# Softmax sums of a whole batch in one PSUM bank by 128x32 column tiles, spread over partitions through DRAM, and fp32 idle matmuls at the front

## The chip, the cores and the metric

The kernel runs on one core of one Trainium2 chip. The metric is the device time of a whole execution in microseconds (us); the number that counts is the median over runs. TensorE is called PE, VectorE DVE, ScalarE ACT, GpSimd POOL and SyncE SP.

## What is computed

A low-rank attention (Linformer) is followed by a feed-forward layer with a maximum over three up projections. All inputs and the output are fp32; the kernel computes in bf16 with fp32 sums.

```
k_proj = einsum('ks,bhsd->bhkd', E, k)       # 1024 keys become 64
v_proj = einsum('ks,bhsd->bhkd', F, v)
scores = (q @ k_proj^T) / 8
attn   = exp(scores - max) / (sum + 1e-9)    # 64 columns per row
x      = attn @ v_proj                       # (b, h, s, d) -> (b s, h d)
out    = max(x @ w1, x @ w2, x @ w3) @ w_out
```

There are 8 batches, 8 heads, 1024 positions, 64 per head; the model width is 512, the hidden width 768. The kernel leaves out the maximum of the scores.

## The kernel before

**Tiling.** Work goes batch by batch. The 8 heads are taken as 4 pairs `g`. For a pair, `scores` (L193) makes the transposed scores of 1024 positions with four 64x64 matmuls into two PSUM banks: partitions hold 64 projected keys for either half `c` of the positions, and the two banks hold the two heads `hp`. ACT writes `pT`, the exponentials in bf16 (`exps`, L208). `sums` (L227) multiplies `pT` with a block of ones, which gives the sums already spread over the 64 partitions of a head, in two banks; `values` (L242) multiplies the same `pT` with the projected values `vp`, in two more banks. Both go through `pair_mm` (L214), four 64x64 matmuls each. `invert` (L230) takes the reciprocal on ACT as Ln and then Exp of the negative, and `scale_x` (L247) multiplies values by it on DVE and writes `xT`, the input of the feed-forward part. `za` issues sums, values, inversion and scaling of a pair together; `sc` issues the scores and puts their Exp into a list, `later`, that is run after the next copy on ACT.

**The feed-forward part** of a batch has two chunks `ch` of 512 positions. `up` (L548) runs 6 steps `jt` of 12 matmuls (L506; three banks, four slices `ct` of `xT` each). The first step of a chunk leaves the last slice of all three banks to its end. ACT copies the first bank (`h1s`, L564), DVE takes two maxima (L568, L516). `down` runs 4 steps `tt` of 6 matmuls (L603); from batch 1 on ACT copies the result to `o_sb`, and SP stores it after every second step.

**Order.** Every engine's instructions run in the order in which the program writes them. `plan(b)` says behind which step of batch `b` the attention work of the next batch is issued: the key `(ch, step)` has steps 0 to 5 for the ups and 6 to 9 for the downs. `kproj`, `vproj` and `kt` make the projected keys and values, `qd` copies the queries on DVE and has SP issue a transposing DMA (L331), `ld` loads a batch through POOL's queue (L189). A planner that runs while the program is built keeps clocks for PE, ACT and DVE and gives each PSUM user the bank that it holds to be free first (`bank`, `two`); on the chip semaphores decide.

**The front.** Until E, F and the first heads have landed, `idle` (L376) issues matmuls on a zeroed tile, `warm`, whose results nobody reads. Batch 0 has an order of its own.

For batches 4 to 7 (`n`), this was the order:

```
        out = {
            (0, 1): [za(n, 0), sc(n, 1)],
            (0, 3): [za(n, 1), sc(n, 2)],
            (0, 9): [za(n, 2), sc(n, 3)],
            (1, 3): [za(n, 3)],
        }
```

Of the kernel before, what the change touches and what calls it, by code (L numbers as in the profile page):

```python
# [15 lines left out]
def kernel(  # L16
# [33 lines left out]
    const = ctx.enter_context(tc.tile_pool(name="const", bufs=1))  # L50
    loads = ctx.enter_context(tc.tile_pool(name="loads", bufs=1))
    att = ctx.enter_context(tc.tile_pool(name="att", bufs=2))
    psum = ctx.enter_context(tc.tile_pool(name="psum", bufs=1, space=bass.MemoryType.PSUM))

    ET = mybir.EngineType
# [61 lines left out]

    ident = const.tile([P, P], BF16, name="ident")
    ones = const.tile([P, HALF], BF16, name="ones")
    warm = const.tile([P, 512], BF16, name="warm")  # L120
    w_sb = [const.tile([P, NCT, DF], BF16, name=f"w{i}_sb") for i in range(3)]
    wout_sb = const.tile([P, NJT, DO], BF16, name="wout_sb")

# [43 lines left out]
    load_kv(2, slice(2, 4))  # L167

    nc.scalar.preload_act_table_set("natural_log_exp_and_others")
    nc.vector.memset(warm, 0.0)  # L170
    make_identity(nc, ident)
    nc.vector.memset(ones, 1.0)

    load_w(0, slice(0, 2))
    load_kv(2, V2)
# [31 lines left out]

    def exps(b, g, lo, nsi, sc):  # L208
        t, ns, ready = sc
        pTs[b, g, lo] = att.tile([P, 2, CHUNK], BF16, name="pT", bufs=4)[:, :, 0:nsi * HALF]  # L210
        nc.scalar.activation(out=pTs[b, g, lo], in_=t, func=AF.Exp, scale=scale)  # L211
        runs("s", ready, 0.17 + nsi * 0.107, ns)

# [13 lines left out]
    def sums(b, g, lo, nsi):  # L227
        return pair_mm(b, g, lo, nsi, lambda rows, hp: ones[rows])

    def invert(b, g, lo, nsi, z):  # L230
        t, ns, ready = z
        zl = att.tile([P, 2, CHUNK], FP32, name="zl", bufs=1)[:, :, 0:nsi * HALF]
        nc.scalar.activation(out=zl, in_=t, func=AF.Ln)  # L233
        runs("s", ready, 0.17 + nsi * 0.107, ns)
        if nsi == SI:
            zi = att.tile([P, 2, CHUNK], FP32, name="zi", bufs=2)
        else:
            zi = att.tile([P, 2, CHUNK // 2], FP32, name="zi0", bufs=4)
        nc.scalar.activation(out=zi, in_=zl, func=AF.Exp, scale=-1.0)  # L239
        zis[b, g, lo] = zi, runs("s", ready, 0.17 + nsi * 0.107)  # L240
# [19 lines left out]
            f()  # L260
        later.clear()

    def sc(b, g, lo=0, nsi=SI):
        def f():
            t = scores(b, g, lo, nsi)
            later.append(lambda: exps(b, g, lo, nsi, t))
        return f

    def za(b, g, lo=0, nsi=SI, then=False):
# [103 lines left out]
        return f  # L373


    def idle(n):  # L376

        t, ns = bank()
        for _ in range(n):
            nc.tensor.matmul(out=t, lhsT=warm[:, 0:P], rhs=warm, start=True, stop=True)  # L380
        free[ns[0]] = pe(n * MM)

    def turn_ef():
        for i in range(2):
# [239 lines left out]
    def plan(b):  # L624
        n = b + 1
        if b == 0:
            c1 = (SPC, SPC)
            return {
                (0, 6): [za(0, 1, *c1), sc(0, 3, *c1)],
                (0, 7): [qd(1, 2), za(0, 2, *c1)],  # L630
                (0, 8): [za(0, 3, *c1)],
                (1, 0): [kproj(1)],
                (1, 1): [kt(1)],
                (1, 2): [vproj(1), ld(2)],
                (1, (3, "mid")): [sc(1, 0), sc(1, 1)],
                (1, 4): [za(1, 0), sc(1, 2)],
                (1, 5): [za(1, 1), sc(1, 3)],
                (1, 7): [za(1, 2)],
                (1, 8): [za(1, 3)],
            }  # L640
# [36 lines left out]
        if n + 2 < B:  # L677
            out[1, 1] += [ld(n + 2)]
        return out
# [61 lines left out]
```

The softmax here doesn't subtract the row's maximum and nothing guards it: scores larger than these inputs give would overflow.

## Time and profile before

| | us |
|---|---|
| median of 10 runs | 405.14 (404.59 to 405.54) |
| the profiled execution | 405.24 |
| its span, first to last instruction | 403.5 |
| PE busy | 394.9 (98%) |
| DVE busy | 202.9 (50%) |
| ACT busy | 189.4 (47%) |
| up matmuls (L506), busy | 258.0 in 1152 |
| down matmuls (L603), busy | 85.6 in 378 |
| sums matmuls (L220, on ones), busy | 13.7 in 144 |

Busy time of an engine is the time in which at least one of its instructions ran. Matmuls overlap, so the duration of one (379 ns for 512 columns) is more than its share of PE's time. In the rows below, a row of a timeline gives start, duration, engine, line, operation, output and inputs, and the count; in brackets stands the idle time before it and what ended it. A row of busy times by stretch gives the stretch, its length, then for PE, PE's weight loads, DVE, ACT and POOL the busy time with the number of instructions, and last PE's clock, the share of the 16 DMA engines and GB/s.

### The profile page before, as it was taken

What the parts mean: (1) busy time and instruction counts of PE and PEld (TensorE: products, weight loads), DVE (VectorE), ACT (ScalarE), POOL (GpSimd) and SP (SyncE); (2) the same over time, 40 slices, a digit from 0 to 9 for tenths busy, and PEclk for the clock granted to TensorE, in tenths of its full rate; (3) what the DMA queues carried; (4) which work ended last, traced back from release to release, by engine and by line L of the source; (5) the groups of instructions that cost most, each with busy time, mean ns of one, the idle gap of its engine ahead of it and who ended that gap; (6) DMA issues with size and microseconds to landing.
All of it is one profiled execution on the core that took longest, in us unless ns stands there. A gap on an engine that the chain in (4) does not pass through costs nothing.

```text
span 403.5 us, 5884 instructions
## 1 busy us (share of the span) xinstructions
PE 394.9 (98%) x2357; PEld 178.5 (44%) x2357; DVE 202.9 (50%) x313; ACT 189.4 (47%) x274; POOL 31.4 (8%) x44
## 2 busy tenths in 40 slices
PE   6999999999999999999999999999999999999996
PEld 2544444444444435444544445444544444444443
DVE  2338755762765527537353655626364363525251
ACT  2531537525672366555643555437535555432322
POOL 7440001001000100200110002000000000000000
PEclk8999999999999999999999999999999999999999
DMA  9999999959907994991799019950510202020202
GB/s 145 206 206 208 233 205 157 241 128 176 237 3 212 191 224 106 154 246 18 210 173 216 29 36 240 205 146 0 145 66 2 104 2 104 2 104 0 106 0 105
DMA packets 62667, 53.33 MB, mean 132 GB/s; under 512 B 30128, under 2 KB 58288, under 8 KB 62640
## 3 DMA queue, kind: packets, MB, share of 16 engines
q0 software_dynamic: 28512, 28.31, 44.3%
q1 hardware_dynamic: 33984, 24.51, 19.8%
q8 instruction: 18, 0.29, 0.3%
q10 hardware_dynamic: 144, 0.13, 0.1%
q14 instruction: 9, 0.07, 0.1%
HBM read 57.15 MB, written 16.78 MB: 183 GB/s over the span
## 4 chain that ended last, share of the span: by engine, by line
PE 92%; ACT 3%; DMA 2%; DVE 2%; issue 1%; SPq 0%; ACTq 0%; DVEq 0%
PE banks L506 61%; PE banks L603 19%; PE banks L220 4%; PE banks L284 3%; PE banks L200 2%; DMA ef_f<-in_F_dram 1%; ACT zl L233 1%; DVE xT L250 1%; ACT zi L239 1%; PE banks L380 1%; PE banks L409 1%; PE banks L295 1%; DMA out_dram<-o_sb 0%; PE banks L435 0%; ACT pT L211 0%
## 5 line engine op out<-in xcount | busy, mean ns | idle before, releaser
L506 PE MATMUL banks<-xT,w_sb 128*128 128x512 bf16 x1152 | 258.0, 379 | 0.4 <-DVE xT L250 0.2
L506 PEld LDWEIGHTS <-w_sb 128*128 128x128 bf16 x1152 | 109.5, 98 | 137.1 <-issue 11.2
L568 DVE TENSOR_TENSOR m<-banks,h1s 128x512 f32<-128x512 f32 x90 | 62.1, 690 | 84.4 <-ACT h1s L564 52.2
L564 ACT COPY h1s<-banks 128x512 f32<-128x512 f32 x90 | 52.5, 583 | 90.3 <-PE banks L506 88.2
L603 PE MATMUL banks<-wout_sb,hT 128*128 128x512 bf16 x378 | 85.6, 379 | 0.0
L250 DVE TENSOR_TENSOR xT<-banks,zi 128x1024 bf16<-128x1024 f32 (+1 forms) x36 | 39.8, 1106 | 73.6 <-ACT zi L239 52.4
L516 DVE TENSOR_TENSOR hT<-banks,m 128x512 bf16<-128x512 f32 x90 | 62.3, 692 | 10.4 <-PE banks L506 1.2
L99 ACT COPY o_sb<-banks 128x512 f32<-128x512 f32 (+1 forms) x56 | 32.6, 581 | 52.2 <-PE banks L603 52.1
L603 PEld LDWEIGHTS <-hT 128*128 128x128 bf16 x378 | 36.0, 98 | 45.2 <-issue 3.1
L233 ACT ACTIVATE zl<-banks 128x1024 f32<-128x1024 f32 (+1 forms) x36 | 33.5, 930 | 31.4 <-PE banks L220 30.5
L211 ACT ACTIVATE pT<-banks 128x1024 bf16<-128x1024 f32 (+1 forms) x36 | 33.2, 930 | 15.9 <-PE banks L200 15.9
L239 ACT ACTIVATE zi<-zl 128x1024 f32<-128x1024 f32 (+1 forms) x36 | 34.6, 962 | 1.1
L189 POOL DMA_DIRECT2D q_t<-in_q_dram x7 | 6.2, 880 | 201.3 <-DMA qT<-q_p 107.2
L220 PE MATMUL banks<-pT,ones 64*64 64x512 bf16 (+1 forms) x144 | 13.7, 374 | 0.7 <-DVE xT L250 0.3
L220 PE MATMUL banks<-pT,vp 64*64 64x512 bf16 (+1 forms) x144 | 13.3, 355 | 0.4 <-DVE vp L99 0.4
L200 PE MATMUL banks<-qT,kpT 64*64 64x512 bf16 (+1 forms) x144 | 13.3, 358 | 0.3 <-DVE m L568 0.3
L284 PEld LDWEIGHTS <-efT 128*64 128x64 bf16 x224 | 11.6, 110 | 3.2 <-issue 2.7
L220 PEld LDWEIGHTS <-ones 64*64 64x64 bf16 x144 | 4.4, 103 | 14.3 <-issue 14.2
L99 DVE CAST vp<-banks 64x256 bf16<-64x256 f32 (+1 forms) x18 | 7.1, 397 | 6.8 <-ACT vp L99 3.5
L99 DVE COPY q_p<-q_t 128x1024 bf16<-128x1024 bf16 x28 | 10.0, 419 | 0.0
L380 PE MATMUL banks<-warm 128*128 128x512 bf16 x21 | 8.5, 527 | 1.2 <-DVE warm L170 1.2
L99 ACT CAST vp<-banks 64x256 bf16<-64x256 f32 x14 | 5.1, 365 | 8.7 <-PE banks L284 8.5
(48 smaller groups left out, 103.3 us busy)
## 6 DMA issues: line engine op xcount, KB each, us to landing
out_dram<-o_sb SPq DMA_DIRECT2D x30, 512.0 KB, 3.5
q_t<-in_q_dram POOLq DMA_DIRECT2D x7, 1024.0 KB, 9.4
k_t<-in_k_dram POOLq DMA_DIRECT2D x7, 1024.0 KB, 13.7
v_t<-in_v_dram POOLq DMA_DIRECT2D x7, 1024.0 KB, 19.0
w_sb<-in_moe_w_dram POOLq DMA_DIRECT2D x5, 384.0 KB, 12.0
k_t<-in_k_dram POOLq DMA_DIRECT2D x2, 512.0 KB, 9.0
v_t<-in_v_dram POOLq DMA_DIRECT2D x4, 256.0 KB, 12.4
wout_sb<-in_moe_w_out_dram POOLq DMA_DIRECT2D x1, 768.0 KB, 15.9
```

The lines of the kernel that those rows point to most:

```text
L99: done = {"v": nc.vector.tensor_copy, "s": nc.scalar.copy, "g": nc.gpsimd.tensor_copy}[eng](out=o, in_=i)
L211: nc.scalar.activation(out=pTs[b, g, lo], in_=t, func=AF.Exp, scale=scale)
L220: nc.tensor.matmul(out=t[hp * HALF:(hp + 1) * HALF, c, 0:nsi * HALF], lhsT=w(rows, hp), rhs=p[rows, hp, :], start=True, stop=True,)
L233: nc.scalar.activation(out=zl, in_=t, func=AF.Ln)
L239: nc.scalar.activation(out=zi, in_=zl, func=AF.Exp, scale=-1.0)
L250: nc.vector.tensor_tensor(out=xTs[b][:, g, lo:lo + nsi, :].rearrange("a (c s) p -> a c (s p)", c=2), in0=t, in1=zi, op=ALU.mult,)
L284: nc.tensor.matmul(out=t[hh * HALF:(hh + 1) * HALF, 0:width], lhsT=efT[:, si, (kv - 1) * KP:kv * KP], rhs=qkv[b][kv][:, heads[hh], si, :], ...
L506: nc.tensor.matmul(out=h, lhsT=w_sb[i][:, ct, jt * P:(jt + 1) * P], rhs=xTs[b][:, ct, ch * SPC:(ch + 1) * SPC, :], start=(ct == first), st ...
L516: nc.vector.tensor_tensor(out=o, in0=h, in1=other, op=ALU.max)
L564: nc.scalar.copy(out=h1s, in_=h[0][0])
L568: nc.vector.tensor_tensor(out=m12, in0=h[1][0], in1=h1s, op=ALU.max)
L603: nc.tensor.matmul(out=o_ps, lhsT=hTs[b, ch][:, jt, tt * P:(tt + 1) * P], rhs=wout_sb[:, jt, :], start=(jt == 0), stop=(jt == NJT - 1),)
```

## The change

Two edits.

At the front, `idle(10)` and `idle(4)` on the bf16 tile become `idle(3, warm_f)` and `idle(1, warm_f)` on an fp32 tile of the same shape, which DVE zeroes first. The planner counts such a matmul as four.

From batch 2 on, the sums of all four pairs are made together by `zc`. A matrix `pick` of zeros and ones has, for either head of a pair, 32 columns of which 8 sum the upper and 8 the lower half of the partitions. Four pairs use the four 32-column tiles of PE and write to the four partition quarters of one bank; the two heads accumulate one after the other. One Ln and one Exp of 128x512 follow on ACT. SP then stores one of every eight equal rows, 16 rows of 2 KB, to a scratch tensor in DRAM, waits for it, and loads it back in two DMAs, one per head half, each read by 64 partitions: 64 x 16 KB, 1 MB each. The result is `zi_all`, of one buffer. `vx` issues the values of a pair and their scaling. The order of work is written anew: the scores of a batch come two or three behind one step, some with their Exp at once (`now=True`), then `zc`, and the values some steps later, two pairs behind one step. `pT` gets six buffers instead of four. Batch 1 still uses `invert`, into a part of its `zi_all`; batch 0 is as before but for the front.

```diff
-        pTs[b, g, lo] = att.tile([P, 2, CHUNK], BF16, name="pT", bufs=4)[:, :, 0:nsi * HALF]
+        pTs[b, g, lo] = att.tile([P, 2, CHUNK], BF16, name="pT", bufs=6)[:, :, 0:nsi * HALF]
...
+    nc.vector.memset(warm_f, 0.0)
     nc.vector.memset(warm, 0.0)
     make_identity(nc, ident)
     nc.vector.memset(ones, 1.0)
+    nc.vector.memset(pick, 0.0)
+    for hp in range(2):
+        for c in range(2):
+            at = hp * 16 + c * 8
+            nc.vector.memset(pick[c * HALF:(c + 1) * HALF, hp, at:at + 8], 1.0)
...
+    def zc(b):
+        def f():
+            t, ns = bank()
+            for hp in range(2):
+                for g in range(NPAIR):
+                    nc.tensor.matmul(
+                        out=t[32 * g:32 * (g + 1), :], lhsT=pick[:, hp, :],
+                        rhs=pTs[b, g, 0][:, hp, :], start=(hp == 0), stop=(hp == 1),
+                    )
+            ready = pe(2 * MM + 0.1)
+            zlc = att.tile([P, CHUNK], FP32, name="zlc", bufs=1)
+            nc.scalar.activation(out=zlc, in_=t, func=AF.Ln)
+            runs("s", ready, 0.6, ns)
+            zic = att.tile([P, CHUNK], FP32, name="zic", bufs=1)
+            nc.scalar.activation(out=zic, in_=zlc, func=AF.Exp, scale=-1.0)
+            when = runs("s", ready, 0.63) + 9.0
+            zd = scratch.tile([NPAIR, 2, 2, CHUNK], FP32, name="zd")
+            nc.sync.dma_start(
+                out=zd.rearrange("g h c f -> (g h c) f"),
+                in_=zic.rearrange("(a r) f -> a r f", r=8)[:, 0, :],
+            )
+            for hp in range(2):
+                nc.sync.dma_start(
+                    out=zi_all(b)[hp * HALF:(hp + 1) * HALF],
+                    in_=zd[:, hp].partition_broadcast(HALF),
+                )
+            for g in range(NPAIR):
+                zis[b, g, 0] = zi_all(b)[:, g], when
+        return f
+
+    def vx(b, g):
+        def f():
+            scale_x(b, g, 0, SI, values(b, g, 0, SI))
+        return f
...
         if nsi == SI:
-            zi = att.tile([P, 2, CHUNK], FP32, name="zi", bufs=2)
+            zi = zi_all(b)[:, g]
...
-    idle(10)
+    idle(3, warm_f)
...
-    idle(4)
+    idle(1, warm_f)
...
-                (0, 7): [sc(2, 0)],
-                (0, 9): [za(2, 0), sc(2, 1)],
-                (1, 1): [za(2, 1), sc(2, 2)],
-                (1, 3): [za(2, 2), sc(2, 3)],
-                (1, 5): [za(2, 3)],
+                (0, 7): [sc(2, 0, now=True), sc(2, 1)],
+                (0, 9): [sc(2, 2, now=True), sc(2, 3)],
+                (1, 0): [zc(2)],
+                (1, 5): [vx(2, 0), vx(2, 1)],
                 (1, 6): [qd(3)],
+                (1, 7): [vx(2, 2), vx(2, 3)],
...
-                (0, 4): [sc(3, 0)],
-                (0, 6): [za(3, 0), sc(3, 1)],
-                (1, 0): [za(3, 1), sc(3, 2), qd(4)],
-                (1, 2): [za(3, 2), sc(3, 3), kproj(4), vproj(4), ld(5)],
+                (0, 4): [sc(3, 0, now=True), sc(3, 1)],
+                (0, 6): [sc(3, 2, now=True), sc(3, 3)],
+                (0, 8): [zc(3)],
+                (1, 0): [qd(4)],
+                (1, 2): [kproj(4), vproj(4), ld(5)],
+                (1, 3): [vx(3, 0), vx(3, 1)],
                 (1, 4): [kt(4)],
-                (1, 5): [za(3, 3), sc(4, 0)],
+                (1, 5): [vx(3, 2), vx(3, 3), sc(4, 0)],
...
-            (0, 1): [za(n, 0), sc(n, 1)],
-            (0, 3): [za(n, 1), sc(n, 2)],
-            (0, 9): [za(n, 2), sc(n, 3)],
-            (1, 3): [za(n, 3)],
+            (0, 1): [sc(n, 1, now=True), sc(n, 2, now=True), sc(n, 3)],
+            (0, 3): [zc(n)],
+            (1, 0): [vx(n, 0), vx(n, 1)],
+            (1, 3): [vx(n, 2), vx(n, 3)],
...
-            out[0, 9] += [kproj(n + 1), vproj(n + 1)]
+            out[1, 0] += [kproj(n + 1), vproj(n + 1)]
```

More of the change, by code (lines that the diff above doesn't have):

```diff
@@ L52 @@
     att = ctx.enter_context(tc.tile_pool(name="att", bufs=2))
+    scratch = ctx.enter_context(
+        tc.tile_pool(name="scratch", bufs=2, space=bass.MemoryType.DRAM)
+    )
     psum = ctx.enter_context(tc.tile_pool(name="psum", bufs=1, space=bass.MemoryType.PSUM))
@@ L119 @@
     ones = const.tile([P, HALF], BF16, name="ones")
+    pick = const.tile([P, 2, 32], BF16, name="pick")
     warm = const.tile([P, 512], BF16, name="warm")
+    warm_f = const.tile([P, 512], FP32, name="warm_f")
     w_sb = [const.tile([P, NCT, DF], BF16, name=f"w{i}_sb") for i in range(3)]
@@ L228, in sums, with zi_all @@
         return pair_mm(b, g, lo, nsi, lambda rows, hp: ones[rows])
+    zi_alls = {}
+    def zi_all(b):
+        if b not in zi_alls:
+            zi_alls[b] = att.tile([P, NPAIR, 2, CHUNK], FP32, name="zi_all", bufs=1)
+        return zi_alls[b]
+    def zc(b):
[23 more added lines that the diff above has]
+                    in_=zd[:, hp].partition_broadcast(HALF),
+                )
+            for g in range(NPAIR):
[5 more added lines that the diff above has]
+        return f
     def invert(b, g, lo, nsi, z):
@@ L261, in run_later, with sc @@
         later.clear()
-    def sc(b, g, lo=0, nsi=SI):
+    def sc(b, g, lo=0, nsi=SI, now=False):
         def f():
             t = scores(b, g, lo, nsi)
-            later.append(lambda: exps(b, g, lo, nsi, t))
+            if now:
+                exps(b, g, lo, nsi, t)
+            else:
+                later.append(lambda: exps(b, g, lo, nsi, t))
         return f
@@ L373, in vproj, with idle @@
         return f
-    def idle(n):
+    def idle(n, w=warm):
         t, ns = bank()
         for _ in range(n):
-            nc.tensor.matmul(out=t, lhsT=warm[:, 0:P], rhs=warm, start=True, stop=True)
-        free[ns[0]] = pe(n * MM)
+            nc.tensor.matmul(out=t, lhsT=w[:, 0:P], rhs=w, start=True, stop=True)
+        free[ns[0]] = pe(n * MM * (4 if w is warm_f else 1))
     def turn_ef():
```

## The prediction

> **What bounds the kernel now.** I read the page first (busy shares, the chain that ended last), then busy time by stretches, then the timeline around one attention stage.
>
> ```profile
> PE 394.9 (98%) x2357; PEld 178.5 (44%) x2357; DVE 202.9 (50%) x313; ACT 189.4 (47%) x274; POOL 31.4 (8%) x44
> ...
> PE 92%; ACT 3%; DMA 2%; DVE 2%; issue 1%; SPq 0%; ACTq 0%; DVEq 0%
> ...
> 80.00:120.00 40.00, 39.70 (x240) 17.82 (x239) 21.49 (x34) 21.00 (x29) 2.63 (x3) 1.00 0.74 143
> 120.00:160.00 40.00, 39.68 (x257) 18.70 (x255) 20.88 (x35) 19.56 (x30) 2.63 (x3) 1.00 0.86 185
> 160.00:200.00 40.00, 40.00 (x244) 18.07 (x242) 20.45 (x32) 22.04 (x31) 2.63 (x3) 1.00 0.76 156
> 200.00:240.00 40.00, 40.00 (x212) 17.55 (x211) 22.02 (x34) 19.65 (x28) 2.63 (x3) 1.00 0.57 108
> ```
>
> In the stretches the first number after the length is PE's busy time. The change acts from about 95 us on, and there PE idles 0.3 us in 80 to 120, 0.3 us in 120 to 160, then not at all. DVE and ACT are half idle. So only two things can move the time: PE work removed, and PE waits created. Time saved on ACT, which the change cuts most, is worth nothing where no PE wait ends on ACT. One stage shows what PE work costs:
>
> ```profile
> 178.01 0.41 PE L220 MATMUL banks<-pT,ones 64*64 64x512 bf16 x4
> ...
> 178.25 0.39 PE L220 MATMUL banks<-pT,vp 64*64 64x512 bf16 x4
> ...
> 178.47 0.39 PE L200 MATMUL banks<-qT,kpT 64*64 64x512 bf16 x4
> 178.53 1.02 ACT L233 ACTIVATE zl<-banks 128x1024 f32<-128x1024 f32 x1 [1.55 <-PE banks L220]
> ...
> 178.79 2.55 PE L506 MATMUL banks<-xT,w_sb 128*128 128x512 bf16 x11
> ```
>
> Four 64x64 matmuls start 0.22 us before the next four: they run side by side, so a group of four is worth 0.22 us. The next stage starts at 184.07, after 24 up matmuls (5.18 us on the chain), so the stage costs 6.06 - 5.18 = 0.88 us: three groups, 0.65, and 0.23 for going into the small tiles and out.
>
> **What the Trainium skill says.** "TensorE: Matmul & The Clock Gate", Part 3 (Packing small matmuls): outputs in different column tiles run concurrently; three 32-column tiles gave 2.38 times. The trace agrees for two column tiles: 32 projection matmuls (L284, 128x64, 256 columns) take 1.87 us, 0.117 a pair. Four are not shown. "SBUF — State Buffer", Door 1: a DMA to 64 partitions reached 196 GB/s at 1 MiB against 328 to 128, and "Can I just issue two DMAs to hit both halves?" says that two such DMAs gain only 6% together. No row here isolates this. "DMA: Bandwidth & Descriptors", Latency and other measured facts: streams whose rows lie at one large pitch in HBM fell to 103 GB/s, half the full rate. Reading one 4 KB row for 64 partitions may resemble that; no row here shows it.
>
> **The change, part by part.**
>
> *Sums on PE.* Removed per batch: four groups of sums, 4 x 0.22. Added: eight 128x32 matmuls in two rounds of four column tiles, 2 x 0.22 if all four run together; bounds 0.43 (as taken) and 8 x 0.216 = 1.73 (one after another). Batches 4 to 7 have four stages before (sums, values, scores) and four after (three scores; the sums; two values with the projections; two values and one scores), so 0.23 x 4 stays. Gain 0.43 a batch, 1.7 us for four.
>
> *Batch 2.* Twelve groups become ten in the same five stages: -0.43. The 0.3 us wait for pT near 98.3 goes. But the last Exp of the scores (1.03) is queued on ACT behind a down copy, another Exp and the h1s copy of an early step, which can start only after its tenth matmul. Laid out from 95.2: the second pair of scores ends at 99.05, the step at 101.65, h1s 101.4 to 102.0, Exp to 103.05, and the new sums need it: 1.3 us of PE wait. Net 1.3 - 0.43 - 0.3 = +0.6.
>
> *Batch 3.* Thirteen groups become eleven, five stages six (+0.23); the 0.3 us near 150.2, where scores waited for a bank, goes; the new sums follow the last scores by two downs and wait about 0.5 for the Exp. -0.43 + 0.23 - 0.3 + 0.5 = 0.
>
> *ACT and DVE.* Per batch four Ln (1.03) and four Exp (1.06) become one of each on 128x512 (0.60, 0.63 in the 128x512 rows): 7.1 us less ACT, hidden anyway. DVE does the same four products (1.23 each), now in pairs: 2.5 us in a step that has 2.59 - 1.38 = 1.2 us of DVE to spare. The banks cover that: after such a pair the next three banks are wanted at 0.9, 1.8 and 2.6 us, and are freed by then; DVE catches up in the next step. Three scores in a row take six banks, which ACT frees at 1.6, 2.6 and 4.2 us, while PE wants banks at 0.9 to 4.4 us: no wait.
>
> *The new wait.* The products now wait for two DMAs. With T the end of step (0,3): sums done T + 0.73, Ln and Exp to T + 2.1, then SP issues the store of 32 KB: nearest row 128 KB, 1.8 us; T + 4.0. SP waits for that landing, then issues two DMAs of 1 MB each to 64 partitions. Their price lies between two ends. As fast as stores: 512 KB lands in 2.6 us against 1.8 for 128 KB, so 2 MB in some 1.4 + 4.8 = 6.2 us. At the skill's rate for half the partitions, 2.1 MB at 208 GB/s (196 plus 6%) = 10.1, with 1.4 of latency 11.5. I take 11.5: landing T + 15.5. A third end is one hot row: at 103 GB/s some 22 us.
>
> Wanted: sums 0.66, two steps and four downs 10.4, step (1,0) 2.59 bring PE to T + 13.65; DVE ends that early step's last maximum 1.95 us later (200.54 to 202.49 in batch 3), so the product wants it at T + 15.6, and some 0.35 us later the projection copy behind it on DVE would hold PE's transposes. For batches 4 to 7, landing 15.5 against 15.6 to 15.95: no wait, but with a margin of under half a microsecond; what comes later than that is paid once a batch, for PE runs out of banks.
>
> *Queues.* Behind SP's waits stand the query transposes (4.0 us of issue) and stores; their data is wanted over 10 us later, o_sb has three buffers. Loads of batches 6 and 7 end before the sums do (DMA share 0.00 at 224 to 236). Not so in batch 2:
>
> ```profile
> 98.00:100.00 2.00, 1.70 (x17) 0.69 (x16) 0.00 (x0) 1.97 (x3) 0.00 (x0) 1.00 1.11 142
> 100.00:102.00 2.00, 2.00 (x11) 0.93 (x10) 0.83 (x1) 1.40 (x3) 0.00 (x0) 1.00 1.13 306
> ...
> 106.00:108.00 2.00, 2.00 (x11) 0.88 (x9) 0.71 (x1) 1.97 (x4) 0.00 (x0) 1.00 1.25 208
> 108.00:110.00 2.00, 2.00 (x11) 0.94 (x10) 1.81 (x4) 1.25 (x2) 0.00 (x0) 1.00 1.20 200
> 110.00:112.00 2.00, 2.00 (x19) 0.71 (x18) 1.38 (x2) 0.80 (x1) 0.00 (x0) 1.00 0.34 58
> ```
>
> The last two columns are DMA share and GB/s: the load of batch 3 keeps the engines full until 111, and stores issued in it took 7.1 to 7.6 us instead of 2.6. Sums end at 103.6, the small store goes out at 105.2, lands about 107.7; 11.5 more and some 1.8 for sharing: 121.0. PE wants it by about 118.5, since two products, four query copies (1.42) and two more products must be through before the next batch's third slice at 123.6. Wait 2.5 us (0 at the fast end, 13 or more at the hot end). Batch 3's transfer starts at 150.9, with the load over: landing 15.7 us after the start of its sums against 15.8. No wait.
>
> *The front.* Ten idle matmuls of 0.43 become three of four passes (four passes for true FP32: "FP8 and Floating Point Precision", TensorE Precision Notes; no row shows one): 12 x 0.43 = 5.1 from about 1.5, so ending by 6.6; the transposes wait for E and F until 7.08 anyway. The single one at 8.45 ends with its cover, the k load at 10.2. PE's clock column reads 0.50 at 9 to 11 us, after 1.9 us of idling; a busier front may avoid that: k_duo took 1.57 against 0.99 later, so 0 to -0.6. Bound the other way +0.6 if these passes keep the clock low for longer. I take -0.2.
>
> **Sum.** -1.7 + 0.6 + 0 + 2.5 - 0.2 = +1.2. The profiled execution took 405.24 (span 403.5), 0.1 above the median of 405.14: 405.14 + 1.2 = **406.3**.
>
> **Rivals.** (a) *The transfer comes in time everywhere*, near the fast end: batch 2's 2.5 goes, -1.3: 403.8, to 403.2 with a warm front. For it: stores move 4 KB pieces at over 400 GB/s. Against: they span 128 partitions. It decides when both DMAs land within 9 us of issue beside a load. (b) *The broadcast is slower than 11.5 us*, by hot rows or the port limit: each microsecond beyond 11.9 costs four batches one each, about as much for batches 2 and 3: 13 us gives 406.3 + 4 x 1.1 + 2.6 = 413; 16 us some 431. For it: a margin of 0.4; against: nothing else runs on the queues then. (c) *Column tiles do not overlap fourfold*: two at a time makes the sums worth nothing, +0.43 a batch, six batches: 409; one at a time 6 x 1.3 = +7.8: 414. Against it: L284. (d) *The front does nothing or harm*: within 0.6 of the forecast.
>
> **Chances.** Forecast as worked 0.40 (403.9 to 408.5 by its own bounds; 0.09 of it within 0.2% of 405.14, the rest slower); (a) 0.25, nearly all faster; (b) 0.27 slower; (c) 0.08, a part cancelled by (a) and so within 0.2%. Of these: faster 0.25, same 0.13, slower 0.62, where 0.2% (0.8 us) is about what a measurement of this kernel can tell from no change. Range 403.2 to 420: it leaves out a wholly warm and early case below and a broadcast of over 14 us above.
>
> **What would show it.** Right: the sums as eight matmuls starting within 0.25 us of each other by fours; the broadcast's time to landing 10 to 13 us; DVE's L250 products waiting on a DMA for 2 to 3 us in batch 2 and hardly later; PE still over 97% busy. Wrong: broadcast under 9 us (rival a), PE waits of over a microsecond at every (1,0) (b), L250 waiting on PE.

## The result and the profile after

The changed kernel is slower: median 417.73 us in 8 runs (416.31 to 418.60) against 405.19 in 29 runs of the kernel before, a ratio of 1.0305 (95% interval 1.0295 to 1.0314). The profiled execution took 417.68 us, its span 415.9.

First the page of the changed kernel: busy time by engine, TensorE's clock in 40 slices, the chain that ended last by engine, and the row of the two loads that spread the inverted sums (`zi_all`, from here on the spread), with the KB of each load and the median us from its issue to its landing.

```profile
PE 394.9 (95%) x2303; PEld 177.0 (43%) x2303; DVE 202.6 (49%) x319; ACT 149.3 (36%) x238; POOL 31.6 (8%) x44
...
PEclk9999999999996999999999999999999999999999
...
PE 62%; DMA 28%; DVE 3%; ACT 2%; issue 2%; POOL 1%; SPq 1%; DVEq 0%; ACTq 0%; POOLq 0%
...
zi_all<-zd SPq DMA_DIRECT2D x12, 1024.0 KB, 11.2
```

ACT has lost 40 us of work, as planned. PE is busy exactly as long as before although it has 54 matmuls less: some of its work ran at a lower clock. And DMA now holds 28% of the chain that ended last, where it held 2%. Not all of that is loss. Two loads of the front (`w_sb` 3.1%, `v_t` 7.2%) make up 10 of the 28 points, and they stand on the chain of e2 as well, which is faster than the kernel before. The spread has 12.8, the query transposes `qT` 3.4, the small store ahead of the spread 1.6. What these cost is read from PE's waits.

The same four stretches as before show where PE stands still; after the stretch and its length the first number is PE's busy time, and the third from the end its clock.

```profile
80.00:120.00 40.00, 38.73 (x222) 17.20 (x221) 17.35 (x29) 14.57 (x24) 2.63 (x3) 1.00 0.97 187
120.00:160.00 40.00, 34.27 (x190) 14.83 (x190) 16.08 (x25) 13.53 (x22) 2.63 (x3) 0.91 0.79 154
160.00:200.00 40.00, 38.95 (x230) 17.31 (x229) 23.00 (x36) 14.21 (x23) 2.63 (x3) 1.00 1.03 198
200.00:240.00 40.00, 36.76 (x217) 16.60 (x215) 18.53 (x29) 12.89 (x22) 2.63 (x3) 1.00 1.07 210
...
120.00:124.00 4.00, 0.00 (x0) 0.00 (x0) 0.00 (x0) 0.25 (x1) 0.00 (x0) 1.00 0.34 78
124.00:128.00 4.00, 2.27 (x12) 0.64 (x12) 3.55 (x6) 0.00 (x0) 0.00 (x0) 0.53 0.00 0
128.00:132.00 4.00, 4.00 (x13) 1.59 (x12) 2.41 (x3) 0.93 (x2) 0.00 (x0) 0.62 0.73 137
```

The loss is not spread over the batches. One hole lies at 120 to 124, a second, in the stretch from 200, at 211.6 to 214.4, and after the first the clock is about half. The timeline of the changed kernel names the instructions behind them; the bracket is the idle time before a row and what ended it.

```profile
102.73 0.59 PE L256 MATMUL banks<-pT,pick 128*32 128x512 bf16 x5 [0.90 <-ACT pT L222]
...
124.45 2.36 DVE L306 TENSOR_TENSOR xT<-banks,zi_all 128x1024 bf16<-128x1024 f32 x2 [7.34 <-DMA zi_all<-zd]
125.72 1.07 PE L231 MATMUL banks<-pT,vp 64*64 64x512 bf16 x8 [6.09 <-DVE xT L306]
...
176.81 0.41 PE L211 MATMUL banks<-qT,kpT 64*64 64x512 bf16 x4 [0.98 <-DMA qT<-q_p]
...
193.67 0.61 PE L256 MATMUL banks<-pT,pick 128*32 128x512 bf16 x8
...
214.40 1.02 PE L565 MATMUL banks<-xT,w_sb 128*128 128x512 bf16 x4 [2.80 <-DVE xT L306]
```

The eight sums matmuls of a batch take 0.61 us (193.67): four column tiles do run together. The product of batch 2 (124.45) waits 7.34 us for its inverses, and PE, out of banks behind it, 6.09 us. The product of batch 4 makes PE wait 2.80. How batch 2 comes to that is read down the chain of waits of the changed kernel (start, duration, what), which follows back from the last instruction to what released it:

```profile
104.65 5.03 DMA zd<-zic
...
110.40 13.93 DMA zi_all<-zd
...
124.45 1.24 DVE xT L306
...
126.79 4.83 PE banks L662 x12
...
162.46 14.31 DMA qT<-q_p
...
201.00 12.00 DMA zi_all<-zd
```

The store of 32 KB needs 5.03 us, the second of the two loads 13.93 from its issue. Then twelve down matmuls take 4.83 us that cost 2.59 elsewhere, at half the clock. The same chain later goes through the query transposes of batch 4, 14.31 us to landing, and the spread of batch 4, 12.00.

The chain also gives a balance between points where a fixed amount of PE work lies: from the first scores of batch 2 (95.23 us before, 95.00 after) to its first up matmul, and from there to the first up matmul of the next batch. The kernels below the second row are the experiments, each read from one profiled execution.

| kernel | batch 2: scores to first up | to batch 3's first up | to batch 4's first up |
|---|---|---|---|
| before | 27.42 | 50.25 | 47.00 |
| after | 36.62 | 50.88 | 50.07 |
| no transfer (e2) | 27.93 | 49.42 | 46.49 |
| spread in bf16 (e7) | 27.98 | 49.44 | 46.49 |
| load of batch 3 left out (e10) | 29.12 | 52.87 | 49.97 |
| part of that load earlier (e5) | 33.81 | 50.92 | 51.62 |
| wait filled (e8) | 33.48 | 52.03 | 53.04 |
| query copies earlier (e6) | 35.09 | 62.31 | 47.34 |
| batches 2 and 3 as before (e3) | 27.43 | 50.25 | 47.10 |
| the same, values later (e9) | 27.42 | 50.25 | 46.60 |

Of the 12.4 us by which the span grew, 9.20 lie in the first column, 0.63 in the second, 3.07 in the third; the stretches after these change by -0.1 together, the front by -0.23. The sum, 12.6, is right to the 0.2 us that such points on the chain are good for.

### The profile page after: what moved, and what is told of

Same layout as the page of the kernel before. It is cut to its first block, busy times and chain, and to the rows that moved or that the text cites. A ratio compares the mean times of both kernels' runs of the same rounds, so it can differ in the third digit from the quotient of the medians.

```text
span 415.9 us, 5769 instructions
## 1 busy us (share of the span) xinstructions
PE 394.9 (95%) x2303; PEld 177.0 (43%) x2303; DVE 202.6 (49%) x319; ACT 149.3 (36%) x238; POOL 31.6 (8%) x44
## 4 chain that ended last, share of the span: by engine, by line
PE 62%; DMA 28%; DVE 3%; ACT 2%; issue 2%; POOL 1%; SPq 1%; DVEq 0%; ACTq 0%; POOLq 0%
PE banks L565 42%; PE banks L662 14%; DMA zi_all<-zd 13%; DMA v_t<-in_v_dram 7%; DMA qT<-q_p 3%; DMA w_sb<-in_moe_w_dram 3%; DVE xT L306 2%; PE banks L211 2%; DMA zd<-zic 2%; PE banks L231 1%; PE banks L343 1%; PE banks L256 1%; ACT zi_all L295 1%; ACT zl L289 1%; SPq L273 1%
## 5 line engine op out<-in xcount | busy, mean ns | idle before, releaser
L662 PE MATMUL banks<-wout_sb,hT 128*128 128x512 bf16 x378 | 88.0, 386 | 0.0
L306 DVE TENSOR_TENSOR xT<-banks,zi_all 128x1024 bf16<-128x1024 f32 x28 | 33.1, 1218 | 20.5 <-DMA zi_all<-zd 15.0
L231 PE MATMUL banks<-pT,vp 64*64 64x512 bf16 (+1 forms) x144 | 11.9, 376 | 6.5 <-DVE xT L306 6.1
L211 PE MATMUL banks<-qT,kpT 64*64 64x512 bf16 (+1 forms) x144 | 11.2, 362 | 1.0 <-DMA qT<-q_p 1.0
L289 ACT ACTIVATE zl<-banks 128x512 f32<-128x512 f32 (+1 forms) x12 | 8.9, 740 | 5.2 <-PE banks L231 4.4
L231 PEld LDWEIGHTS <-vp 64*64 64x64 bf16 x144 | 3.5, 106 | 13.1 <-issue 11.4
L102 DVE COPY o_sb<-banks 128x512 f32<-128x512 f32 (+1 forms) x9 | 5.8, 654 | 4.5 <-PE banks L642 4.5
L343 PE MATMUL banks<-v_t,efT 128*64 128x256 bf16 x112 | 7.3, 273 | 0.3 <-DMA v_t<-in_v_dram 0.3
L343 PE MATMUL banks<-k_t,efT 128*64 128x256 bf16 x112 | 7.5, 276 | 0.0
## 6 DMA issues: line engine op xcount, KB each, us to landing
w_sb<-in_moe_w_dram POOLq DMA_DIRECT2D x5, 384.0 KB, 12.8
```

The costliest lines, as they stand in the source:

```text
L102: done = {"v": nc.vector.tensor_copy, "s": nc.scalar.copy, "g": nc.gpsimd.tensor_copy}[eng](out=o, in_=i)
L211: nc.tensor.matmul(out=t[c * HALF:(c + 1) * HALF, hp, 0:n * P], lhsT=kpTs[b][rows, g, :], rhs=qTs[b][rows, at:at + n, :], start=True, stop ...
L231: nc.tensor.matmul(out=t[hp * HALF:(hp + 1) * HALF, c, 0:nsi * HALF], lhsT=w(rows, hp), rhs=p[rows, hp, :], start=True, stop=True,)
L306: nc.vector.tensor_tensor(out=xTs[b][:, g, lo:lo + nsi, :].rearrange("a (c s) p -> a c (s p)", c=2), in0=t, in1=zi, op=ALU.mult,)
L343: nc.tensor.matmul(out=t[hh * HALF:(hh + 1) * HALF, 0:width], lhsT=efT[:, si, (kv - 1) * KP:kv * KP], rhs=qkv[b][kv][:, heads[hh], si, :], ...
L662: nc.tensor.matmul(out=o_ps, lhsT=hTs[b, ch][:, jt, tt * P:(tt + 1) * P], rhs=wout_sb[:, jt, :], start=(jt == 0), stop=(jt == NJT - 1),)
```

## The experiments

**e1_front.** The kernel before with the front alone changed.

```diff
-    idle(10)
+    idle(3, warm_f)
...
-    idle(4)
+    idle(1, warm_f)
```

> The kernel before with only the fp32 idle matmuls. In the profile of the changed kernel the projection of the first keys starts 0.64 us earlier, but batch 1's first scores come only 0.23 us earlier (95.00 against 95.23). Theory: the rest of the front waits for loads, so 405.0, -0.2 (between -0.5 and 0). Rival: the front is worth what it saves at its first step, -0.6 to -1.2: 404.0 to 404.6. Second rival, that it harms: above 405.4.

Measured: 405.41 us (21 runs) against 405.10 (27), ratio 1.0009 (1.0002 to 1.0015). The expected gain is not there. The first two lines are of the timeline of e1_front, the last of its busy times by stretch:

```profile
1.46 5.49 PE L382 MATMUL banks<-warm_f 128*128 128x512 f32 x6 [1.46 <-DVE warm_f L171]
...
9.45 1.03 PE L411 MATMUL banks<-k_t,efT 128*64 128x256 bf16 x8 [0.20 <-DMA k_t<-in_k_dram]
```

```profile
9.00:11.00 2.00, 1.80 (x12) 0.99 (x11) 0.54 (x2) 0.00 (x0) 0.57 (x2) 1.00 1.35 203
```

An fp32 matmul appears as two instructions, so three are six. They took 5.49 us here and 4.48 in the changed kernel, where the prediction had 5.1 from four passes. The clock at 9 to 11 us is 1.00 where it was 0.50, and the first key projection starts at 9.45 instead of 10.26. That head start comes to nothing. Spans agree within 0.1 us (medians 403.4 and 403.3); that the work behind it waits for loads was the theory and is not shown. The rest of the 0.3 us lies outside the span, 2.02 us against 1.77. The other kernels with the same fp32 front, the changed one among them, have 1.7 to 1.8 there, so this rest is not shown to be the front's, and its cause stays open.

**e2_no_spread.** The changed kernel without its three transfers per batch.

```diff
-            zd = scratch.tile([NPAIR, 2, 2, CHUNK], FP32, name="zd")
-            nc.sync.dma_start(out=zd..., in_=zic...)
-            for hp in range(2):
-                nc.sync.dma_start(out=zi_all(b)..., in_=zd...)
...
-                zis[b, g, 0] = zi_all(b)[:, g], when
+                zis[b, g, 0] = zi_one, when
```

> The changed kernel without the store of the inverted sums and without the two loads that spread them: from batch 2 on the values are multiplied by a constant 1/64 instead. All matmuls, Ln and Exp stay, and the order of work. Theory: the loss is the transfer, by waiting and by what it displaces on the DMA queues; without it the new order is worth -0.43 in each of six batches, +1.2 for the sums of batches 2 and 3 that wait for an Exp, -0.6 for old waits gone and -0.2 for the front: 405.1 - 2.2 = 402.9 (402.3 to 404.0). Rival: the new order of scores and values itself stalls PE, through banks or DVE: 408 or more.

Measured: 403.26 (4 runs), ratio 0.9958 (0.9945 to 0.9971). The change without its transfers is a gain, and the whole loss, 14.5 us, belongs to the transfers or to what they hold up.

**e3_old_2_3.** Batches 2 and 3 ordered as before, batches 4 to 7 as changed.

```diff
-                (0, 7): [sc(2, 0, now=True), sc(2, 1)],
-                (0, 9): [sc(2, 2, now=True), sc(2, 3)],
-                (1, 0): [zc(2)],
-                (1, 5): [vx(2, 0), vx(2, 1)],
+                (0, 7): [sc(2, 0)],
+                (0, 9): [za(2, 0), sc(2, 1)],
+                (1, 1): [za(2, 1), sc(2, 2)],
+                (1, 3): [za(2, 2), sc(2, 3)],
+                (1, 5): [za(2, 3)],
...
```

> The changed kernel with the order of work of the kernel before for batches 2 and 3 (sums per pair, inverted in place); only batches 4 to 7 use the spread sums. Theory: 9 of the 12.5 us were lost in batch 2 and 3 in batch 4 by a chain that began in batch 3 (query transposes behind the spread, then the load of batch 5 17 us later, then the spread of batch 4 beside that load). With both batches as before, the load of batch 5 starts at 160 to 162, batch 4's small store lands in 1.8 instead of 4.7, and batches 4 to 6 pay about 0.6 of wait each against 0.43 gained, batch 7 nothing: 405.1 - 0.2 + 3 x 0.17 - 0.43 = 405.0 (404.3 to 405.6). Rival: each batch with a spread costs about 2 us whatever its neighbours do: 411.

Measured: 406.58 (6 runs), ratio 1.0045 (1.0032 to 1.0058). It lies 1.6 us above the expected 405.0, outside its range, and far from the rival: most of the loss comes with batches 2 and 3, and batch 4's stretch, too, is almost as before once they are (47.10). What is left shows in the timeline of e3_old_2_3:

```profile
203.13 0.29 PE L410 MATMUL banks<-ident,kp 128*128 128x128 bf16 x2 [0.43 <-DVE kp L102]
...
296.75 1.02 PE L565 MATMUL banks<-xT,w_sb 128*128 128x512 bf16 x4 [0.71 <-DVE xT L306]
```

With no load beside it, the store lands in 1.8 us and the second load in 11.8 to 11.9 after its issue. The product then waits about 1 us, the copy of the keys stands behind it on DVE, and PE's transposes lose 0.43 to 0.44 us in batches 4, 5 and 6.

**e4_shapes.** As e3, with other sources and targets for the two loads of 1 MB in batches 5 to 7, to price the spread by itself.

```diff
+                if b == 5:      # distinct rows, 64 partitions each
+                    o, x = full[i * HALF:(i + 1) * HALF], q[0, 4 * i:4 * i + 4]...
+                elif b == 6:    # one row for all, 128 partitions each
+                    o, x = zi_all(b)[:, 2 * i:2 * i + 2], zd[2 * i:2 * i + 2, 0].partition_broadcast(P)
+                elif b == 7:    # distinct rows, 128 partitions each
+                    o, x = full[:, 2 * i:2 * i + 2], q[0, 4 * i:4 * i + 4]...
```

> As the run with batches 2 and 3 as before, with other sources for the two 1 MB loads, 4 KB pieces in all: batch 4 as in the change (one row for 64 partitions), batch 5 rows of the input q, each read once, to 64 partitions, batch 6 one row for 128 partitions, batch 7 rows of q, each read once, to 128 partitions. Batches 5 to 7 thus multiply by wrong numbers. Read is the time to landing of the second load after the issue of the first, 12.6 in the changed kernel. Theory: the limit is the half of the partitions: 12.6, 12.6, about 7, about 7. Rival: reading one row many times is the limit: 12.6, 7, 12.6, 7. Second rival: 4 KB pieces from HBM are that slow in any shape: 12 to 13 in all four.

Measured: 404.1 in one run; what counts here is not this time but the landings. Three rows on the loads of e4_shapes, with the time from each issue to its landing, for batch 5, batch 6 and batch 7:

```profile
DMA to landing us min/median/max: 7.5/9.6/11.6
...
DMA to landing us min/median/max: 6.2/7.7/9.3
...
DMA to landing us min/median/max: 5.4/6.5/7.5
```

The largest is the second load of a pair (11.9 in batch 4); it is issued 0.5 to 0.7 us after the first. From the first issue, 2 MB take 12.6 us as the change does it (batch 4), 12.3 with distinct rows, 9.8 with one row for 128 partitions, 8.0 with distinct rows for 128. Half the partitions cost 4.3 us with distinct rows and 2.8 with one row, one row for many 0.3 to 1.8. Each shape was measured once, in a batch of its own. Batch 7 differs from the others in that no query transposes follow on SP, but in that place the change's own form took 12.5 us (e3), so the place does not make the difference.

**e5_load_early.** A second key buffer (and one buffer less for `pT`), so that part of batch 3's load could go out long before batch 2's store.

```diff
-            for nm, n in (("q_t", 2), ("k_t", 1), ("v_t", 1))
+            for nm, n in (("q_t", 2), ("k_t", 2), ("v_t", 1))
...
-                (0, 1): [qd(2)],
-                (0, 5): [kproj(2), vproj(2), ld(3)],
+                (0, 1): [qd(2), ld(3)],
+                (0, 5): [kproj(2), vproj(2)],
```

> The changed kernel with the load of batch 3 started earlier: a second buffer for k, k loaded before q, the load issued behind step (0,1) of batch 1 instead of (0,5) (pT gets five buffers, for room). In the changed kernel the small store of batch 2 took 5.0 us and the spread 14.6 beside this load. Theory: what batch 2 loses beyond the forecast is the company of the load. With the load done by about 104, the store lands in 1.8 to 2.5 and the spread 12.6 later, at about 119.3 instead of 124.3; the product waits about 2 instead of 7.3 us, PE stalls 1 instead of 6.1 and its clock does not fall: 417.7 - 5.1 - 2.7 = 410 (409 to 411.5). Rival: the store and the spread are as slow without the load, since reads of rows just written are slow: 416 or more.

Measured: 416.14 (4 runs), ratio 1.0268 (1.0250 to 1.0287): a miss. The keys went out at 62.0, but queries and values only at 93.0 and 93.8, and the values landed at 111.2 instead of 112.9. So the load was not out of the way, the store still took 4.74 us, and the experiment did not test what it was for. What it shows is small: a load that ends 1.7 us earlier brought the spread 2.1 us earlier (122.2 against 124.3).

**e6_query_copies_early.** The query copies and transposes of batch 4 moved ahead of batch 3's store and spread on SP.

```diff
                 (0, 4): [sc(3, 0, now=True), sc(3, 1)],
+                (0, 5): [qd(4)],
                 (0, 6): [sc(3, 2, now=True), sc(3, 3)],
                 (0, 8): [zc(3)],
-                (1, 0): [qd(4)],
```

> The changed kernel with the query copies and the transposing DMA of batch 4 issued behind step (0,5) of batch 2 instead of (1,0), so ahead of the spread of batch 3 on SP's queue. Theory: the chain behind batch 4's loss starts with these transposes standing behind the spread. Ahead of it they land in 6 to 8 instead of 14.3 us, the load of batch 5 starts its queries by 160 instead of 177 and is over before batch 4's sums, whose store lands in 1.8 instead of 4.7; batch 4's 3.1 us and the 1.0 us wait for the queries go, but the spread of batch 3 now shares with that load and may cost 0 to 2 us: 413.6 to 415.6. Rival: batch 4's loss comes from elsewhere: 417 to 418, store still 4 us or more.

Measured: 424.41 (4 runs), ratio 1.0479 (1.0456 to 1.0503), worse than the change by 7. The load of batch 5 did start early again (161.2 us, 177.3 in the changed kernel), but batch 3's spread was issued at 162.1 and so ran beside it. One line of the chain of e6_query_copies_early, and one of its timeline:

```profile
162.72 17.38 DMA zi_all<-zd
```

```profile
181.50 0.37 PE L410 MATMUL banks<-ident,kp 128*128 128x128 bf16 x2 [10.00 <-DVE xT L306]
```

PE waited 10.00 us, and its clock then stayed at 0.50 until 187.2. In the table the second column rises by 11.4, while the third falls to 47.34, and batch 4's store lands in 1.8 us. So batch 4's loss in the changed kernel came from its displaced load, and putting that load back moves the collision to batch 3 instead of ending it.

**e7_spread_bf16.** Inverses rounded to bf16 before they are stored and spread, so half the bytes.

```diff
-            zi_alls[b] = att.tile([P, NPAIR, 2, CHUNK], FP32, name="zi_all", bufs=1)
+            zi_alls[b] = att.tile([P, NPAIR, 2, CHUNK], BF16, name="zi_all", bufs=1)
...
-            zic = att.tile([P, CHUNK], FP32, name="zic", bufs=1)
+            zic = att.tile([P, CHUNK], BF16, name="zic", bufs=1)
...
-            zd = scratch.tile([NPAIR, 2, 2, CHUNK], FP32, name="zd")
+            zd = scratch.tile([NPAIR, 2, 2, CHUNK], BF16, name="zd")
```

> The changed kernel with the inverted sums in bf16: half the bytes in the store and in the spread (2 KB pieces), all else alike. Theory: bytes into half of the partitions set the latency, so the second load lands about 7 us after the first is issued instead of 12.6; every wait of batches 4 to 7 goes (-0.6 in three, so the gain of 0.43 shows), batch 2's spread lands at about 118 and PE stalls little, the clock stays up: 403.5 to 405. Rival: the latency is by pieces, not bytes (the number of pieces is the same): 12 us again, 417.

Measured: 402.92 (7 runs), ratio 0.9954 (0.9937 to 0.9971), faster than both kernels. The two loads of batch 2 in e7_spread_bf16, from issue to landing, still with batch 3's load beside the store, which takes 4.7 us although it too has half the bytes:

```profile
DMA to landing us min/median/max: 7.6/7.9/8.1
```

They land at 118.4 us, before the product wants them. In the table e7 agrees with e2 to 0.05 us: the transfer has become free, and no clock is lost. Apart from the sums' 0.90 us for the last Exp, no wait of PE over 0.3 us is left after 95 us.

**e8_wait_filled.** 26 idle bf16 matmuls in the changed kernel's wait of batch 2, to keep PE's clock.

```diff
-                (1, 7): [vx(2, 2), vx(2, 3)],
+                (1, 7): [lambda: idle(26), vx(2, 2), vx(2, 3)],
```

> The changed kernel with 26 idle bf16 matmuls (5.6 us at full clock) put ahead of the last two values of batch 2, into the 6.1 us in which PE waits for the spread. Theory: PE's clock fell to 0.5 after that wait, and the twelve down matmuls that follow took 4.83 us instead of 2.59, the values 1.07 instead of 0.56; with PE kept busy the clock stays at 1.00: 417.7 - 2.7 = 415.0 (414.5 to 415.6). Rival: the slow downs came from something else, such as DVE or bank waits: 417.7 or, with fillers in the way, more.

Measured: 419.46 (4 runs), ratio 1.0352 (1.0322 to 1.0383): a miss in the total, a hit in the place. Two stretches of e8_wait_filled:

```profile
124.00:128.00 4.00, 4.00 (x25) 1.63 (x24) 4.00 (x8) 0.59 (x1) 0.00 (x0) 1.00 0.00 1
...
212.00:216.00 4.00, 2.78 (x9) 1.08 (x9) 3.92 (x6) 0.00 (x0) 0.10 (x1) 0.50 1.21 336
```

The clock stays at 1.00 at 124 to 128, and the first column is 3.14 us shorter: values and downs take 0.56 and 2.70 us instead of 1.07 and 4.83, which is 2.6, and the other 0.5 comes with a spread that landed 1.4 us earlier, which the fillers do not explain. But batch 3's store, now 3.3 us earlier, meets the load of batch 4, which ends at 156.8 as it did (156.4): it takes 3.7 us instead of 1.8, PE waits 2.29 for the product, and in batch 4 it waits 3.81 and the clock falls there. So the lost clock is real, some 2.6 us, but time won ahead of a transfer is not time won. About 1.7 us more is lost in the later batches; a wait of 1.27 in batch 5 is part of it, the rest is open.

**e10_no_load_3.** The changed kernel with batch 3's load left out; batch 3 works on batch 2's tiles.

```diff
     def load(b):
+        if b == 3:
+            qkv[3] = qkv[2]
+            return
         tiles = load_tiles(b)
```

> The changed kernel, with the load of batch 3 left out: batch 3 works on the query, key and value tiles of batch 2, so that no load runs beside batch 2's store and spread. Theory: that load is what makes them late. The store then lands in 1.8 us instead of 5.0 and the spread as in batches 5 and 6 (12.6 us after its first issue), some 120 us into the span instead of 124.3; TensorE waits 1 us or less instead of 6.1 and its clock stays at 1.00 through 124 to 131 us, where it was 0.50. That is 5 + 2.75 us, while the loss of batch 4 stays: 409.7 us (408.0 to 411.5), ratio about 1.011. Rival: the spread is slow by itself, wherever it runs; it lands after 123 us as before, TensorE waits over 4 us, and the time is 415.5 or more.

Measured: 414.33 (4 runs), ratio 1.0212 (1.0184 to 1.0240). The time lies 2.8 us above the expected range: a miss in the size. The mechanism is there. Lines of the chain of e10_no_load_3, then of its timeline:

```profile
104.85 1.79 DMA zd<-zic
...
107.36 12.24 DMA zi_all<-zd
```

```profile
121.01 0.63 PE L234 MATMUL banks<-pT,vp 64*64 64x512 bf16 x8 [1.18 <-DVE xT L309]
...
167.96 0.27 PE L413 MATMUL banks<-ident,kp 128*128 128x128 bf16 x2 [2.90 <-DVE xT L309]
```

Without the load the store lands in 1.79 instead of 5.03 us, the spread at 119.6 instead of 124.3, PE waits 1.18 instead of 6.09, and the first column falls by 7.5 us. As in e8 a part is given back at once: batch 3's store meets batch 4's load, and PE waits 2.90 there. The profiled execution, which these lines and the table show, was the fastest of the four: 412.26 us, with a mean clock of 1.00. The other three had 0.992 to 0.995 and took 414.05 to 414.76, so the same kernel lost clock in some executions and not in others; where, their records do not show.

**e11_by_pair.** The spread cut by pairs: four loads that write all 128 partitions each, from two rows.

```diff
-            for hp in range(2):
-                nc.sync.dma_start(
-                    out=zi_all(b)[hp * HALF:(hp + 1) * HALF],
-                    in_=zd[:, hp].partition_broadcast(HALF),
-                )
+            for g in range(NPAIR):
+                nc.sync.dma_start(
+                    out=zi_all(b)[:, g].rearrange("p c f -> p (c f)"),
+                    in_=zd[g].rearrange("h c f -> h (c f)").unsqueeze(1).broadcast_to([2, HALF, 2 * CHUNK]),
+                )
```

> The changed kernel with the spread cut the other way: four transfers of one pair each that write all 128 partitions, instead of two that write 64 each; same bytes, same fp32 values, nothing left out. Theory: writing 64 partitions at a time is what made the price 12.6 us instead of under 10. The last of the four lands 8 to 10.5 us after the first issue in batches 4 to 7, products there wait for nothing, and in batch 2, beside the load, it lands by 121.5 us, so that TensorE waits 2 us or less and keeps its clock: 404.3 us (403.0 to 406.5), ratio about 0.998. Rival: the repeated reading of one row in DRAM sets the rate, or four issues on SP take what is gained; landings stay at 12 us and above, and the time is 413 or more.

Measured: 579.10 (6 runs), ratio 1.4281 (1.4251 to 1.4310). A stretch of e11_by_pair in which PE waits for the spread; the last two columns are the share of the 16 DMA engines and GB/s:

```profile
140.00:150.00 10.00, 3.15 (x7) 1.01 (x7) 1.23 (x1) 0.00 (x0) 0.00 (x0) 0.67 0.13 52
```

A share of 0.13 is two engines of sixteen, at 52 GB/s; the four loads took some 40 us. The source's outermost count here is 2 (the heads), where it was 64. The Trainium skill, "DMA: Bandwidth & Descriptors", Why a DMA increments its semaphore by 16 and not by 1, says that the number of engines, up to 16, has to divide the count of the slowest dimension; the trace agrees, two for a count of 2. So the run tests that and not the partitions, and whether a spread over all 128 would help inside the kernel stays open.

**e12_bf16_old_front.** e7 with the bf16 front of the kernel before.

```diff
-    idle(3, warm_f)
+    idle(10)
...
-    idle(1, warm_f)
+    idle(4)
```

> The changed kernel with both findings: inverses stored and spread as bf16, and the idle matmuls at the front as bf16 ones again (10 and 4). The spread in bf16 alone gave 402.92, and the fp32 front alone cost 0.3 us on the kernel before. Theory: the two are independent, 402.6 us (402.2 to 403.0), ratio about 0.994, better than both kernels by over 0.4%. Rival: the front is worth nothing here, 402.9 to 403.3.

Measured: 402.61 (6 runs), ratio 0.9935 (0.9916 to 0.9954). This is the lowest median of all versions. It is 0.3 us below e7, but the two intervals overlap and the two ran on different chips, so that the old front is better is not shown.

**e9_later_values.** e3 with the first two products of a batch one step later.

```diff
-            (1, 0): [vx(n, 0), vx(n, 1)],
+            (1, 0): [],
+            (1, 1): [vx(n, 0), vx(n, 1)],
...
-            out[1, 1] = [kt(n + 1)]
+            out[1, 1] = [kt(n + 1)] + out[1, 1]
```

> As e3_old_2_3 (batches 2 and 3 in the old order, 406.58 us), with one thing moved: from batch 4 on the first two products with the values stand one step later in the second half, after the key and value projections of the next batch. Theory: what is left of the loss in batches 4 to 7 is only that the spread lands some 1 us after the product wants it, and that the copy of the keys stands behind that product on VectorE (waits of TensorE of 0.44 us in three batches, 0.71 more in one). With the product later both go: 404.2 us (403.2 to 405.0), ratio about 0.998. Rival: the chain only moves, the products now come too late for the first up matmuls of the batch, and TensorE waits there instead: 406.5 us or more.

Measured: 403.94 (6 runs), ratio 0.9971 (0.9958 to 0.9983), 2.6 us below e3: all waits of PE of over 0.33 us after 95 us are gone, with fp32 inverses. One step of room is enough for a spread that has the queues for itself, as it has here, where batches 2 and 3 do without one.

## Why the prediction was right or wrong

The side was right, the size was not: +1.2 us was the forecast, +12.5 the measurement. That 417.7 still lies inside the range of 403.2 to 420 is luck: the range reached so far up for rival (b), a spread of 13 to 14 us that is paid in every batch, and the loss came another way, in batches 2 and 4 through other loads on the queues. Of the prediction's own signs the eight sums matmuls and the 10 to 13 us to landing came true; a product that waits 2 to 3 us in batch 2 (it was 7.34) and PE over 97% busy (it was 95) did not. Step by step:

**Sums on PE: right.** 0.43 us saved per batch was forecast; without the transfer batch 4's stretch is 0.51 shorter (e2, third column), and in the changed kernel itself the stretch of batch 7, where PE waits for nothing, is 0.45 shorter. Four column tiles overlap fourfold, so rival (c) is out.

**Batch 2's and 3's order: right and too careful.** Forecast +0.6 and 0; without the transfer +0.51 and -0.83. The sums waited 0.90 for the last Exp (1.3 forecast).

**The price of the spread: near.** Forecast 11.5 us from the first issue, measured 12.6 with free queues. The basis, a lower rate into 64 partitions than into 128 (the Trainium skill, "SBUF — State Buffer", Door 1: 196 against 328 GB/s at 1 MiB, a factor of 1.67), holds in e4: 12.3 us against 8.0 for the same 2 MB of distinct rows, a factor of 1.54. Rival (b) put a loss on every batch from this price; in batches 5 to 7 it is 0.44, 0.44 and 0, because in these batches the product's lateness reaches PE only through the key copy behind it, which batch 7 does not have.

**Batch 2's wait: the term that was mis-sized.** Forecast 2.5, measured 6.09 of standing still plus some 2.75 of slow clock (4.83 + 1.07 us where 2.59 + 0.56 is usual). Two steps of its sum failed. "Lands about 107.7" for the small store: it landed at 109.68. It had been given 2.5 us where it took 5.03, although the prediction itself had stores of 512 KB at 7.1 to 7.6 us beside that load instead of 2.6. And "some 1.8 for sharing": the second load landed 14.6 us after the first issue, 13.3 had been allowed. Together that is 3.3 us, 124.3 instead of 121.0. The clock had no term at all. e10 shows that the load is the cause of the store's delay, e8 that the wait is the cause of the clock. By what means a load holds up a store of 32 KB stays open.

What the store does beside a load is seen best side by side (us into the span):

| store of | issued | landed | last load then running, landed |
|---|---|---|---|
| after, batch 2 | 104.65 | 109.68 | 112.9 |
| after, batch 3 | 156.67 | 158.49 | none (the last one at 156.4) |
| after, batch 4 | 195.6 | 200.3 | 200.7 |
| e10, batch 2 | 104.85 | 106.64 | none |
| e10, batch 3 | 149.4 | 153.6 | 153.5 |

With queues free it takes 1.8 us whatever the kernel, beside a load 4.2 to 5.0 in these rows; two of the three landed within half a microsecond of the load's own end. In the other experiments it took 3.7 to 4.9 beside a running load, and 2.0 to 2.8 where a load was just ending or had just begun.

**Batch 3: right by luck.** The prediction had its transfer start "with the load over". It did, but only because batch 2 had lost 9 us: the store went out at 156.67, and batch 4's load had landed at 156.4. Where batch 2 loses little, the two meet: in e7 the store went out at 148.2 and took 4.6 us beside that load, in e10 at 149.4 with 4.2, and there PE waited 2.90 for the product. So this wait, too, was put at nothing wrongly.

**Queues: the step that failed outright.** "Behind SP's waits stand the query transposes (4.0 us of issue) and stores; their data is wanted over 10 us later" costed this at nothing. The transposes of batch 4 went out right behind the spread, held SP for 12.29 us instead of 3.99 and landed after 14.31; PE waited 0.98 for them. Worse, POOL's load of batch 5 waits for these transposes. The first line is of the timeline of before, the others of the changed kernel:

```profile
160.78 0.88 POOL L189 DMA_DIRECT2D q_t<-in_q_dram  x1 [27.30 <-DMA qT<-q_p]
...
162.46 12.29 SPq L390 DMA_TRANSPOSE qT<-q_p  x1
...
177.32 0.88 POOL L200 DMA_DIRECT2D q_t<-in_q_dram  x1 [34.87 <-DMA qT<-q_p]
```

So it started 16.5 us late and ran beside batch 4's store and spread, for which the prediction had taken free queues (it looked only at the loads of batches 6 and 7). That is batch 4's +3.07, and e6 shows both sides of it.

**The front: no gain.** -0.2 forecast, +0.3 measured in e1, of which 0.1 lies in the span and the rest is not shown to be the front's. The clock column did what was hoped for; nothing of it was left at the end.

## What to carry to other kernels

A small transfer on the path is priced by what runs beside it, not by its bytes: 1.8 us became 5, and where the work ahead got faster (e8, e10) the next transfer met the next load. Before moving a result through DRAM, lay its store and its load on the same time line as every bulk load, and follow what is queued behind them to the load that this delays. Then buy slack where it is cheap: half the bytes (e7), or one step of later use where the queues are free (e9), each turned a loss into a gain of 0.3 to 0.5%.

## What was not expected of the hardware

**The clock falls and returns in steps.** Read in stretches of 0.4 us, it stood at half for 6.8 us in the changed kernel (124.25 to 131.07), twice 3.4 us in e5, 6.8 in e8, 3.4 and 10.2 in e6: one, two or three times 3.4. The Trainium skill, "TensorE: Matmul & The Clock Gate", Part 1, names a free-running window of 3.413 us, and the traces agree with it. They also show what a fall costs here: after the wait of 6.09 us it was some 2.75 more. How short a wait can be is not sharp: one of 2.75 us in e5 was followed by a fall, one of 2.80 in the changed kernel and one of 2.90 in e10 were not.

**A transposing DMA holds its issuer longer behind other transfers.** The same instruction kept SP for 3.94 to 4.12 us before (from 80 us on) and, in batches 4 to 7 of the changed kernel, where it goes out right behind a spread, for 9.7 to 14.1.

**The order of an access pattern is a price.** e11 moved 52 GB/s with two engines busy; 2.1 MB in the 12 us of the form with 64 as its outermost count are 175.
